# Second layer norm of a transformer block, tile by tile beside the output projection: one change to a single-core kernel

## Chip, core and metric

The kernel runs on one core of a Trainium2 chip. TensorE multiplies matrices, VectorE, ScalarE and GpSimd work beside it, SyncE issues the DMAs. Each engine takes its own instructions strictly in program order. The metric is device time in microseconds from launch to end.

## What is computed

One block over 2048 rows of 512, with 32 heads of 16, an FFN of 1792 and six modulation vectors made from c. In the kernel all products are made of fp32 parts (a high part, and a low part that is the rest).

```
mod = (silu(c) @ w_mod) -> sa, ca, ga, sb, cb, gb
h = layernorm(x) * (1 + ca) + sa
x = x + ga * (softmax(q k^T * scale) v) @ wo        # q, k, v = h @ wqkv, per head
h = layernorm(x) * (1 + cb) + sb
x = x + gb * (gelu(h @ w1 + b1) @ w2 + b2)
```

## The kernel before

Attention goes through 32 units (four blocks of 512 query rows, eight groups of four heads) of 16 key steps each. The main loop runs over these 512 **half steps** (`half_step`). Each one puts on TensorE four score tiles (`e`, line 637), four score tiles for row maxima of a later unit (`mx`, line 387) and, at its end, the four products with v of an earlier half step (`pv`, line 667). ScalarE takes the exponential of each `e` (line 642), VectorE the maximum of each `mx` (line 392). Scores contract over at most 64 rows, so two of them, or a score and a half of another product, run in the two halves of the array at a time.

Everything else is **background work**: the jobs of `work()`, of which a half step takes up to six half-array matmuls (`RUN = 6`, named `bg`, line 274), in one PSUM bank. They are, in this order, the remaining projections (`block0`), and then for query blocks 0, 1 and 2 the `front` (output projection, residual, second layer norm, transposes) and the `feed` (FFN). A job that isn't ready yields `None`: that half step has no background work and counts as idle below. Jobs that are left when the loop ends run in the **tail**, as full-array matmuls, one after the other; the fourth block's front and feed are made there by code of their own, which the change doesn't touch.

Order is set by a counter, not by time. Every `e` raises `clock["t"]` by one (a **tick**; four in a half step), and `later(n, f)` writes f's instructions n ticks further on. In the tail every second matmul is a tick.

`front(b, x2)` makes four output tiles of 128 rows (24 half matmuls, so four half steps each). For each, ScalarE copies the result out (`y`), two ticks later GpSimd adds the residual into `x2[t]`, and four ticks later VectorE takes the statistics (`ln_stat`: BN_STATS, BN_AGGR). After the last tile came one `ln_factor` for all four (VectorE adds eps, GpSimd raises to the power -0.5) and the four normalisations `xn[t]`, and the generator waited until 21 ticks were over, before `trans` turned `xn` on TensorE in four half steps (four transposes each, no other background work). Block 0's front stands alone between the projections and its FFN. The fronts of blocks 1 and 2 are put ahead of the last four groups of the FFN before them, so that their waits pass under those groups.

Of the kernel before, what the change touches and what calls it, by code (L numbers as in the profile page):

```python
# [8 lines left out]
F32 = mybir.dt.float32  # L9
FR = mybir.dt.float32r  # L10
AF = mybir.ActivationFunctionType
ALU = mybir.AluOpType
# [4 lines left out]
P = 128  # L17
# [15 lines left out]
EPS = 1e-5  # L33
# [36 lines left out]
def block_kernel(ctx: ExitStack, tc: tile.TileContext, x, wqkv, wo, w1, b1, w2, b2, c, w_mod, out):  # L70
    nc = tc.nc
    te, ve, ac, gp, sy = nc.tensor, nc.vector, nc.scalar, nc.gpsimd, nc.sync
# [21 lines left out]
    def take(name):  # L94
        ids = rings[name]
        turn[name] += 1
        return bank(ids[(turn[name] - 1) % len(ids)], name)
# [14 lines left out]
    small = ctx.enter_context(tc.tile_pool(name="small", bufs=2))  # L112
# [4 lines left out]
    mhalf = const.tile([P, NB], F32, name="mhalf")  # L117
# [7 lines left out]
    b2_b = const.tile([P, D], F32, name="b2_b")  # L125
# [107 lines left out]
    def ln_stat(mv, t, rows):  # L233
        st = small.tile([P, 6], F32, tag="bst", name="bst")
        ve.bn_stats(st, rows)  # L235
        ve.bn_aggr(mv[:, t], st)

    def ln_factor(mv, rs):
        ve.tensor_scalar(rs, mv[:, :, 1], EPS, None, op0=ALU.add)
        gp.tensor_tensor(rs, rs, mhalf, op=ALU.pow)  # L240
# [5 lines left out]
    clock = {"t": 0}  # L246
    hooks = {}

    def later(n, f):
        if n:  # L250
            hooks.setdefault(clock["t"] + n, []).append(f)
        else:
            f()
# [315 lines left out]
    for token in SCRIPT.split():  # L569
        name, ids, e, n = re.fullmatch(r"([A-Za-z]+)(\d*)(?:\.([avg]))?(?:\*(\d+))?", token).groups()  # L570
# [121 lines left out]
    def pc(b, k, a, sl=slice(None)):  # L692
        return pc_t[k][:, a, sl] if b == NB - 1 else pcs[a][:, k, sl]

    def tmp(name):
        if "f" in pools:
            return pools["f"].tile([P, D], F32, tag="t", name=name, bufs=8)
        return dvpool.tile([P, D], F32, tag="t", name=name, bufs=4)
# [50 lines left out]
    def until(cond):  # L749
        while not cond():  # L750
            yield None

    def wait(n):
        t0 = clock["t"]
        return until(lambda: clock["t"] >= t0 + n)
# [30 lines left out]
    def loaded(b, *keys):  # L786
        return until(lambda: all((b, *k) in wt for k in keys))

    def drop(b, *keys):
        used.update((b, *k) for k in keys)  # L790
# [3 lines left out]
    def o_terms(b, t, ks):  # L794
        sl = slice(t * P, (t + 1) * P)
        return [(pc(b, k, a, sl), wt[b, "o", k][:, c]) for k in ks for a, c in three]

    def load_x2(b, x2):
        for t in range(4):
            r0 = b * TB + t * P  # L800
            sy.dma_start(x2[t], x[r0 : r0 + P, :])

    def front(b, x2):


        later(9, lambda: load_x2(b, x2))
        yield from until(lambda: done[b] == KC - 1)
        yield from wait(4)
        yield from loaded(b, *[("o", k) for k in range(KC)])
        mv = small.tile([P, 4, 2], F32, tag="mv", name="mv")  # L810
        rs = small.tile([P, 4], F32, tag="rs", name="rs")
        for t in range(4):

            def evac(ps, t=t):
                y = tmp("y")
                ac.activation(y, ps, AF.Copy)  # L816

                def add():
                    gp.tensor_tensor(x2[t], y, x2[t], op=ALU.add)  # L819
                    later(4, lambda: ln_stat(mv, t, x2[t]))  # L820

                later(2, add)

            yield o_terms(b, t, range(KC)), "bg", evac
        drop(b, *[("o", k) for k in range(KC)])
        later(9, lambda: ln_factor(mv, rs))
        xn = []

        def norm(t):
            (gp if b or t in (0, 2) else ve).tensor_scalar(  # L830
                xn[t], x2[t], mv[:, t, 0:1], rs[:, t : t + 1], op0=ALU.subtract, op1=ALU.mult)

        def norms():
            xn.extend(tmp("xn") for t in range(4))
            for t in range(4):
                later(3 * (t == 3), lambda t=t: norm(t))
                later(28 + 12 * t, lambda t=t: gp.tensor_tensor(x2[t], x2[t], b2_b, op=ALU.add))

        later(13, norms)
        t0 = clock["t"]  # L840
        yield "ln"
        yield from until(lambda: clock["t"] >= t0 + 21)

        def trans(fc):
            ps = take("bg")
            for t in range(4):
                te.transpose(ps[:, t * P : (t + 1) * P], xn[t][:, fc * P : (fc + 1) * P], ident)  # L847
            h = tmp("h32")
            ac.activation(h, ps, AF.Identity, scale=modc[:, 1, fc, 0:1], bias=modc[:, 1, fc, 1:2])  # L849
            gp.tensor_copy(pc(b, fc, 0), h)  # L850
            gp.tensor_tensor(pc(b, fc, 1), h, pc(b, fc, 0).bitcast(F32), op=ALU.subtract)

        for fc in range(KC):
            yield lambda fc=fc: trans(fc)
        yield from wait(4)
# [103 lines left out]
    def work():  # L959

        yield from block0()
        fronts = [front(b, pools["x2"][b % 2]) for b in range(NB - 1)]
        for b in range(NB - 1):
            for j in fronts[b]:
                if j != "ln":
                    yield j
            for j in feed(b, pools["x2"][b % 2]):
                if j != "last":
                    togo[0] -= b == NB - 2 and j is not None
                    yield j  # L970
                elif b < NB - 2:
                    for i in fronts[b + 1]:
                        if i == "ln":
                            break
                        yield i
# [125 lines left out]
    x2 = [tpool.tile([P, D], F32, name=f"x2t{i}") for i in range(4)]  # L1101
# [21 lines left out]
    mv = small.tile([P, 4, 2], F32, tag="mv", name="mv")  # L1123
    rs = small.tile([P, 4], F32, tag="rs", name="rs")
    xn = [tmp("xn") for t in range(4)]
# [97 lines left out]
```

## Time and profile before

| | us |
|---|---|
| median of 3 runs | 1738.71 (1736.97 to 1739.3) |
| the profiled execution | 1738.16 |
| its span, first to last instruction | 1736.3 |
| TensorE, VectorE, ScalarE, GpSimd busy | 1710.8, 1375.2, 1241.8, 685.0 |

A row of the timeline has the start, the duration, the engine, the line, and what was written from what; "x8" counts instructions merged into one row, and brackets hold the idle time just ahead and what ended it. One `pv` product counts as two instructions there. The time from one `pv` row to the next is one half step. PEld is TensorE's weight load. The granted TensorE clock is 0.997 of full speed over the span.

### The profile page before, as it was taken

To read this page: it belongs to the slowest core of one execution; us is meant where nothing else is said; L and a number is where in the kernel's file an instruction comes from. 1 tells how busy PE (TensorE), PEld (TensorE's weight loads), DVE (VectorE), ACT (ScalarE), POOL (GpSimd) and SP (SyncE) were. 2 spreads that over 40 slices of the span, in tenths; PEclk is the share of its full clock that TensorE was granted. 3 is DMA by queue.
4 is the path that set the end of the run, shared out by engine and by line. 5 is a ranking of instruction groups with operands and counts; after the bars stand their busy time and mean duration, and the time that the engine had idled before them with its cause. 6 is when DMAs were issued, how large, how long until landed. Compare 5 with 4: busy or idle time off the path is not lost.

```text
span 1736.3 us, 32537 instructions
## 1 busy us (share of the span) xinstructions
PE 1710.8 (99%) x12121; PEld 891.1 (51%) x12121; DVE 1375.2 (79%) x2298; ACT 1241.8 (72%) x2379; POOL 685.0 (39%) x688
## 2 busy tenths in 40 slices
PE   7999999999999999999999999999999999999999
PEld 6654444444444444444445444444445444444777
DVE  7998888888888888888889888888888888860332
ACT  3357778778777778778777778777877778778231
POOL 7333434435121256404631356404631356525310
PEclk8999999999999999999999999999999999999999
DMA  8646776767447534335454444335364344323554
GB/s 292 205 142 200 221 218 182 236 179 223 125 136 206 125 86 117 94 85 136 113 168 106 124 114 105 94 81 166 100 174 114 101 132 114 97 66 111 195 156 166
DMA packets 137130, 251.90 MB, mean 145 GB/s; under 512 B 25854, under 2 KB 45324, under 8 KB 136972
## 3 DMA queue, kind: packets, MB, share of 16 engines
q1 hardware_dynamic: 135712, 248.19, 50.3%
q8 instruction: 96, 1.57, 0.4%
q10 hardware_dynamic: 1260, 1.63, 0.3%
q14 instruction: 62, 0.51, 0.1%
HBM read 188.49 MB, written 61.28 MB: 144 GB/s over the span
## 4 chain that ended last, share of the span: by engine, by line
PE 91%; DVE 4%; ACT 2%; POOL 1%; DMA 1%; issue 1%; SPq 0%; ACTq 0%; POOLq 0%; DVEq 0%
PE bg L274 46%; PE pv L667 29%; PE e L637 11%; PE mx L387 3%; DVE mxp L392 2%; ACT p L642 1%; PE pr L274 1%; PE o L274 1%; PE warm L438 1%; DVE hTlo L481 1%; DVE bst L235 0%; ACT h L849 0%; DMA qst<-m 0%; PE mx L333 0%; PE bg L847 0%
## 5 line engine op out<-in xcount | busy, mean ns | idle before, releaser
L392 DVE TENSOR_REDUCE mxp<-mx 128x1 f32<-128x512 f32 x2048 | 1269.4, 682 | 201.4 <-PE mx L387 182.5
L642 ACT ACTIVATE p<-e 128x512 f32<-128x512 f32 x2032 | 1064.4, 605 | 308.1 <-PE e L637 292.8
L387 PE MATMUL mx<-kh,qst 48*128 48x512 f32 x2048 | 873.3, 441 | 1.9 <-DVE mxp L392 0.4
L637 PE MATMUL e<-qst,kh 50*128 50x512 f32 x2032 | 754.6, 419 | 7.0 <-ACT p L642 6.3
L667 PE MATMUL pv<-p,vg 128*32 128x512 f32 x4096 | 546.6, 605 | 0.0
L637 PEld LDWEIGHTS e<-qst,kh 50*128 50x128 f32 x2032 | 373.7, 186 | 148.7 <-ACT p L642 141.8
L387 PEld LDWEIGHTS mx<-kh,qst 48*128 48x128 f32 x2048 | 368.6, 185 | 21.1 <-DVE mxp L392 16.2
L274 PE MATMUL bg<-w,g 64*128 64x512 f32 (+1 forms) x1044 | 277.8, 404 | 0.0
L274 PEld LDWEIGHTS bg<-w,g 64*128 64x128 f32 (+1 forms) x1044 | 183.0, 185 | 142.7 <-ACT p L642 103.3
L274 PE MATMUL bg<-pchi,w 64*128 64x512 f32 (+1 forms) x656 | 194.5, 416 | 2.1 <-ACT p L642 2.0
L274 PEld LDWEIGHTS bg<-pchi,w 64*128 64x128 f32 (+1 forms) x656 | 109.0, 184 | 150.3 <-ACT p L642 102.2
L274 PE MATMUL bg<-hThi,wqkv 64*128 64x512 f32 x560 | 167.4, 418 | 0.3 <-ACT p L642 0.3
L274 PEld LDWEIGHTS bg<-hThi,wqkv 64*128 64x128 f32 x560 | 92.8, 184 | 118.9 <-ACT p L642 106.3
L667 PEld LDWEIGHTS pv<-p,vg 128*32 128x32 f32 x4096 | 81.4, 108 | 125.4 <-issue 117.6
L884 POOL TENSOR_SCALAR s<-s 128x512 f32<-128x512 f32 x40 | 59.8, 1496 | 137.4 <-ACT s L882 127.0
L903 POOL TENSOR_TENSOR x<-y,x 128x512 f32<-128x512 f32 x28 | 35.9, 1281 | 144.3 <-ACT y L902 139.3
L274 PE MATMUL bg<-pclo,w 64*128 64x512 f32 (+1 forms) x328 | 88.6, 389 | 0.0
L872 DVE TENSOR_TENSOR g<-h,g 128x512 fp32r<-128x512 f32 x16 | 11.6, 723 | 91.5 <-PE bg L274 62.7
L274 PE MATMUL bg<-hTlo,wqkv 64*128 64x512 f32 x280 | 76.4, 392 | 0.0
L819 POOL TENSOR_TENSOR x<-y,x 128x512 f32<-128x512 f32 x12 | 15.4, 1282 | 140.9 <-ACT y L816 114.8
L274 PEld LDWEIGHTS bg<-pclo,w 64*128 64x128 f32 (+1 forms) x328 | 60.5, 184 | 12.3
L274 PE MATMUL bg<-wo,pchi 64*128 64x512 f32 x192 | 64.8, 417 | 0.0
(160 smaller groups left out, 1331.9 us busy)
## 6 DMA issues: line engine op xcount, KB each, us to landing
kh<-qk SPq DMA_DIRECT2D x256, 192.0 KB
w<-w1s SPq DMA_DIRECT2D x56, 512.0 KB
w<-w2s SPq DMA_DIRECT2D x53, 512.0 KB
vg<-v SPq DMA_DIRECT2D x64, 332.0 KB
qk<-parts SPq DMA_DIRECT2D x32, 512.0 KB
qst<-qk SPq DMA_DIRECT2D x64, 192.0 KB
qk<-parts SPq DMA_DIRECT2D x32, 256.0 KB
ou<-osb SPq DMA_DIRECT2D x32, 256.0 KB
```

The source lines that it names most:

```text
L274: return te.matmul(ps, term[0][r], term[1][r], start=i == 0, stop=i == n - 1)
L387: te.matmul(ps, qst[u][r0 : r0 + KR, p, qc * P : (qc + 1) * P], kh(u, kr // 2)[r0 : r0 + KR, p, (kr % 2) * TB : (kr % 2 + 1) * TB], start= ...
L392: ins = ve.tensor_reduce(mxp[u][:, hc, kr : kr + 1], ps, axis=AX.X, op=ALU.max, negate=True)
L438: te.matmul(warm[:, :P], ident, ident, start=True, stop=True)
L481: e.tensor_tensor(hT[b][1][:, f], keep.pop(("H", b, f)), hT[b][0][:, f].bitcast(F32), op=ALU.subtract)
L637: te.matmul(ps, kh(u, kc // 8)[r0 : r0 + KX, p, (kc % 8) * P : (kc % 8 + 1) * P], qst[u][r0 : r0 + KX, p], start=True, stop=True)
L642: saw(ac.activation(t, ps, AF.Exp, scale=SCALE))
L667: te.matmul(cur["ps"][32 * j : 32 * (j + 1)], vg[u][:, kc, j * VW : j * VW + 32], pt.pop(4 * s + j), start=kc == 0, stop=kc == NKC - 1)
L819: gp.tensor_tensor(x2[t], y, x2[t], op=ALU.add)
L872: ve.tensor_tensor(g[:, 1], h, g[:, 0].bitcast(F32), op=ALU.subtract)
L884: gp.tensor_scalar(s, s, 1.0, None, op0=ALU.add)
L903: later(4, lambda: gp.tensor_tensor(x2[t], y, x2[t], op=ALU.add))
```

## The change

Each tile gets statistics, factor and normalisation of its own as soon as it is there. The factors are four 128x1 tiles (`rt`) in place of one 128x4. Tiles 0 to 2 are normalised by GpSimd, tile 3 by VectorE, in every block (before: block 0 by GpSimd for tiles 0 and 2 and VectorE for 1 and 3, the other blocks by GpSimd alone). The last tile's steps follow each other one tick sooner. The transposes come when all four tiles are written and nine ticks are over. The adding of b2 to `x2[t]` now comes 40 ticks after the tile's normalisation.

```
-        rs = small.tile([P, 4], F32, tag="rs", name="rs")
+        def norm(t):
+            xn[t] = tmp("xn")
+            (gp if t < 3 else ve).tensor_scalar(
+                xn[t], x2[t], mv[:, t, 0:1], rs[t], op0=ALU.subtract, op1=ALU.mult)
+            later(40, lambda: gp.tensor_tensor(x2[t], x2[t], b2_b, op=ALU.add))
+        def stat(t):
+            ln_stat(mv, t, x2[t])
+            later(2 if t < 3 else 1, lambda: factor(t))
+        def factor(t):
+            rs[t] = small.tile([P, 1], F32, tag=f"rt{t}", name=f"rt{t}")
+            ve.tensor_scalar(rs[t], mv[:, t, 1:2], EPS, None, op0=ALU.add)
+            gp.tensor_tensor(rs[t], rs[t], mhalf[:, 0:1], op=ALU.pow)
+            later(3 if t < 3 else 2, lambda: norm(t))
...
-                    later(4, lambda: ln_stat(mv, t, x2[t]))
+                    later(4 if t < 3 else 3, lambda: stat(t))
...
-        later(9, lambda: ln_factor(mv, rs))
-        def norm(t):
-            (gp if b or t in (0, 2) else ve).tensor_scalar(
-                xn[t], x2[t], mv[:, t, 0:1], rs[:, t : t + 1], op0=ALU.subtract, op1=ALU.mult)
-        def norms():
-            xn.extend(tmp("xn") for t in range(4))
-            for t in range(4):
-                later(3 * (t == 3), lambda t=t: norm(t))
-                later(28 + 12 * t, lambda t=t: gp.tensor_tensor(x2[t], x2[t], b2_b, op=ALU.add))
-        later(13, norms)
...
-        yield from until(lambda: clock["t"] >= t0 + 21)
+        yield from until(lambda: len(xn) == 4 and clock["t"] >= t0 + 9)
```

VectorE in block 0's front, from the statistics of tile 3 (`x_7490`) on. First before, then changed; `mxp` rows are the row maxima of the main loop, `mn` the end of a unit's maxima:

```order
L235 BN_STATS bst<-x_7490 128x6
L236 BN_AGGR mv<-bst 128x2
L392 TENSOR_REDUCE mxp<-mx 128x1 x5
L239 TENSOR_SCALAR rs<-mv 128x4
L392 TENSOR_REDUCE mxp<-mx 128x1 x4
L830 TENSOR_SCALAR xn<-x_7488,mv,rs 128x512
L392 TENSOR_REDUCE mxp<-mx 128x1 x3
L830 TENSOR_SCALAR xn<-x_7490,mv,rs 128x512
```

In the changed kernel:

```order
L235 BN_STATS bst<-x_7490 128x6
L236 BN_AGGR mv<-bst 128x2
L392 TENSOR_REDUCE mxp<-mx 128x1
L826 TENSOR_SCALAR rt_8356<-mv 128x1
L392 TENSOR_REDUCE mxp<-mx 128x1 x2
L816 TENSOR_SCALAR xn<-x_7490,mv,rt_8356 128x512
```

Tile 3 is normalised after three maxima in place of twelve, and tile 1's normalisation has left VectorE.

GpSimd at the same place, from the residual add of tile 3 on, before:

```order
L819 TENSOR_TENSOR x_7490<-y,x_7490 128x512
L240 TENSOR_TENSOR rs<-rs,mhalf 128x4
L830 TENSOR_SCALAR xn<-x_7487,mv,rs 128x512
L830 TENSOR_SCALAR xn<-x_7489,mv,rs 128x512
L850 CAST pchi_5322<-h_8532 128x512
```

And changed, where `b_b` is b2 over all rows and the `xn` rows of tiles 0 to 2 stand further up, each behind its own add:

```order
L837 TENSOR_TENSOR x_7490<-y,x_7490 128x512
L818 TENSOR_TENSOR x_7487<-x_7487,b_b 128x512
L827 TENSOR_TENSOR rt_8356<-rt_8356,mhalf 128x1
L854 CAST pchi_5322<-h_8439 128x512
L855 TENSOR_TENSOR pclo_5323<-h_8439,pchi_5322 128x512
```

Between the add and the cast that follows the first transposes, GpSimd now has one add of b2 and one 128x1 power.

TensorE where the main loop ends and the tail begins. Before: the last two `pv` products stand together, and two FFN groups of 12 (`pchi`, `pclo`) follow:

```order
L274 MATMUL bg<-pclo_5323,w_22538 128x512 x3
L637 MATMUL e<-qst,kh_192 128x512
L667 MATMUL pv<-p,vg 32x512 x8
L274 MATMUL bg<-pchi_5322,w_22566 128x512 x8
L274 MATMUL bg<-pclo_5323,w_22566 128x512 x4
L274 MATMUL bg<-pchi_5322,w_22629 128x512 x8
L274 MATMUL bg<-pclo_5323,w_22629 128x512 x4
L274 MATMUL bg<-w_22693,g 128x512 x3
```

Changed:

```order
L637 MATMUL e<-qst,kh_192 128x512 x2
L667 MATMUL pv<-p,vg 32x512 x4
L274 MATMUL bg<-pchi_5322,w_22563 128x512 x2
L274 MATMUL bg<-pclo_5323,w_22563 128x512 x4
L667 MATMUL pv<-p,vg 32x512 x4
L274 MATMUL bg<-pchi_5322,w_22620 128x512 x8
L274 MATMUL bg<-pclo_5323,w_22620 128x512 x4
L274 MATMUL bg<-w_22688,g 128x512 x3
```

Of the two FFN groups one has gone into the loop, but for its last six half matmuls, which now stand alone between the last two `pv` products. In the rows of TensorE as a whole, block 0 has three idle half steps between its projection and its first transposes where it had six; the idle half steps of the other two blocks are as many as before, and stand three half steps sooner.

More of the change, by code (lines that the diff above doesn't have):

```diff
@@ L810, in front @@
         mv = small.tile([P, 4, 2], F32, tag="mv", name="mv")
-        rs = small.tile([P, 4], F32, tag="rs", name="rs")
+        rs = {}
+        xn = {}
+        def norm(t):
[11 more added lines that the diff above has]
+            later(3 if t < 3 else 2, lambda: norm(t))
         for t in range(4):
@@ L825, in front @@
         drop(b, *[("o", k) for k in range(KC)])
-        later(9, lambda: ln_factor(mv, rs))
-        xn = []
-        def norm(t):
-            (gp if b or t in (0, 2) else ve).tensor_scalar(
-                xn[t], x2[t], mv[:, t, 0:1], rs[:, t : t + 1], op0=ALU.subtract, op1=ALU.mult)
-        def norms():
-            xn.extend(tmp("xn") for t in range(4))
-            for t in range(4):
-                later(3 * (t == 3), lambda t=t: norm(t))
-                later(28 + 12 * t, lambda t=t: gp.tensor_tensor(x2[t], x2[t], b2_b, op=ALU.add))
-        later(13, norms)
         t0 = clock["t"]
         yield "ln"
-        yield from until(lambda: clock["t"] >= t0 + 21)
+        yield from until(lambda: len(xn) == 4 and clock["t"] >= t0 + 9)
         def trans(fc):
```

## The prediction

> **What bounds the kernel now.** I read the page first: its engine totals, then the chain that ended last.
>
> ```profile
> PE 1710.8 (99%) x12121; PEld 891.1 (51%) x12121; DVE 1375.2 (79%) x2298; ACT 1241.8 (72%) x2379; POOL 685.0 (39%) x688
> PE 91%; DVE 4%; ACT 2%; POOL 1%; DMA 1%; issue 1%; SPq 0%; ACTq 0%; POOLq 0%; DVEq 0%
> ```
>
> TensorE carries 91% of the chain. So a wait that is taken out pays only by what TensorE has less to do, or waits less, afterwards. Next I took TensorE's timeline around block 0's front, keeping the `pv` rows, one for each half step. The first two bound a half step with background work; from 585.23 on there is none, until the transposes.
>
> ```profile
> 561.71 1.06 PE L667 MATMUL pv<-p,vg 128*32 128x512 f32 x8
> 564.63 1.07 PE L667 MATMUL pv<-p,vg 128*32 128x512 f32 x8
> ...
> 585.23 1.06 PE L667 MATMUL pv<-p,vg 128*32 128x512 f32 x8
> 587.97 1.06 PE L667 MATMUL pv<-p,vg 128*32 128x512 f32 x8
> 591.15 1.06 PE L667 MATMUL pv<-p,vg 128*32 128x512 f32 x8
> 593.89 1.07 PE L667 MATMUL pv<-p,vg 128*32 128x512 f32 x8
> ...
> 602.32 1.07 PE L667 MATMUL pv<-p,vg 128*32 128x512 f32 x8
> 603.33 0.65 PE L847 MATMUL bg<-ident,xn 128*128 128x128 f32 x4
> ```
>
> A half step with background work takes 564.63 - 561.71 = 2.92 us, an idle one 587.97 - 585.23 = 2.74: an idle half step is nearly as long as a full one. The six idle ones take 602.32 - 585.23 = 17.09 us. The one that holds tile 3's statistics takes 3.18. So what is lost in an idle half step is not its 2.74 us, but six half matmuls that must be done later. Where they are done is the tail. The timeline there, all engines, at the first groups of FFN weights `w` with `g`:
>
> ```profile
> 1677.96 16.50 PE L274 MATMUL bg<-w,g 128*128 128x512 f32 x72
> ```
>
> 72 full matmuls in 16.50 us, 0.229 each, with no wait inside. VectorE's rows from the front to the transposes, and one half step of the loop without a front:
>
> ```profile
> 588.60 0.68 DVE L235 BATCH_NORM_STATS2 bst<-x 128x6 f32<-128x512 f32 x1
> 589.32 0.18 DVE L236 BATCH_NORM_AGGREGATE mv<-bst 128x2 f32<-128x6 f32 x1
> 592.38 0.16 DVE L239 TENSOR_SCALAR rs<-mv 128x4 f32<-128x4 f32 x1
> 595.12 0.54 DVE L830 TENSOR_SCALAR xn<-x,mv,rs 128x512 f32<-128x512 f32 x1
> 597.37 0.54 DVE L830 TENSOR_SCALAR xn<-x,mv,rs 128x512 f32<-128x512 f32 x1
> ...
> 1300.39 2.48 DVE L392 TENSOR_REDUCE mxp<-mx 128x1 f32<-128x512 f32 x4 [0.43 <-PE mx L387]
> ```
>
> Four maxima take 2.48 us, and VectorE then waits 0.43 for TensorE: that is the room for layer-norm work in a full half step.
>
> **The change, part by part.** By the rows of the changed program, three of block 0's six idle half steps go. All later background work comes three half steps, that is 18 half matmuls, sooner. Twelve of them are half of an FFN group, six more stand at the loop's end, and the tail loses that one group of 12 full matmuls.
>
> *Tail.* 12 x 0.229 = -2.75 us.
>
> *Loop.* The three idle half steps that stay hold tile 3's statistics, factor and one normalisation. I take 2.74 + 3.18 + 2.85 = 8.77 for them (the last with 0.11 for a normalisation, from the other half steps of the six: 17.09 - 2.74 - 3.18 - 2.74 = 8.43 for three with two normalisations in them). So 17.09 - 8.77 = 8.32 go, and three full ones come, 3 x 2.92 = 8.76: +0.44. Bounds 0 to +0.6.
>
> *The end of the loop.* ScalarE's second half of the GELU is written ten ticks behind its FFN group. TensorE's and ScalarE's rows there:
>
> ```profile
> 1605.66 1.11 PE L667 MATMUL pv<-p,vg 128*32 128x512 f32 x8
> 1607.80 0.62 ACT L882 ACTIVATE s<-s 128x512 f32<-128x512 f32 x1
> 1608.38 1.06 PE L667 MATMUL pv<-p,vg 128*32 128x512 f32 x8
> 1611.61 2.67 PE L667 MATMUL pv<-p,vg 128*32 128x512 f32 x16
> 1613.22 0.14 PEld L667 LDWEIGHTS pv<-p,vg 128*32 128x32 f32 x4 [0.61 <-ACT p L642]
> 1614.21 2.11 PE L274 MATMUL bg<-pchi,w 128*128 128x512 f32 x8
> ```
>
> Behind that tanh the half step takes 1611.61 - 1608.38 = 3.23 in place of 1608.38 - 1605.66 = 2.72, since no maxima are left and the exponentials set the pace. Shifted by three half steps, one more of them falls into the loop: +0.51 (0 to +1.0).
>
> *The six half matmuls left over.* They stand between the last two `pv` products and run alone in half the array. The spacing of background matmuls and the turn from and to `pv`, in TensorE's rows ahead of the 564.63 above:
>
> ```profile
> 562.71 0.50 PE L274 MATMUL bg<-wo,pchi 64*128 64x512 f32 x1
> ...
> 563.04 0.39 PE L274 MATMUL bg<-wo,pchi 64*128 64x512 f32 x1
> ...
> 563.28 0.39 PE L274 MATMUL bg<-wo,pclo 64*128 64x512 f32 x1
> ...
> 564.22 0.48 PE L387 MATMUL mx<-kh,qst 48*128 48x512 f32 x1
> ```
>
> One goes each 0.24 us (563.28 - 563.04); the first after `pv` takes 0.33, the last before `pv` 0.41. Six alone: 0.33 + 4 x 0.24 + 0.41 = 1.7 us. Part of this covers what TensorE now spends waiting there: the last two `pv` take 2.67 against two at 1.06, 0.55 of waiting, with the exponential there at 1613.2. That leaves +1.1 (0 if the wait hides more than I see, +1.7 if none). The Trainium skill, TensorEngine Tiling (Array Packing), Key Properties, says that a change of tiling mode drains TensorE. The trace agrees: 0.33 and 0.41 at the turns against 0.24 between; without the drain this term would be 6 x 0.24 - 0.55 = +0.9 and the sum 0.2 lower.
>
> *VectorE, other blocks.* Each front gets three more small factor ops and blocks 1 and 2 a normalisation that GpSimd had. Their statistics rest in full half steps:
>
> ```profile
> 917.33 1.07 PE L667 MATMUL pv<-p,vg 128*32 128x512 f32 x8
> 920.34 1.06 PE L667 MATMUL pv<-p,vg 128*32 128x512 f32 x8
> ```
>
> With statistics of 0.68 + 0.18 the half step takes 3.01, 0.09 more than 2.92, though VectorE had only 0.43 free: the rest is taken up by its lag. Nine factor ops of 0.16 each and two normalisations of 0.54 are 2.5 us of VectorE work; tile 3's come within two half steps (0.86 + 0.16 + 0.54 = 1.56 against 2 x 0.43), so there I take 0.3 a block. Sum +0.6 (0 to 2.5).
>
> *GpSimd and the order in queues.* The rows of before, and those of the factors by tile:
>
> ```profile
> 585.81 1.28 POOL L819 TENSOR_TENSOR x<-y,x 128x512 f32<-128x512 f32 x1 [10.50 <-ACT y L816]
> 592.62 1.04 POOL L240 TENSOR_TENSOR rs<-rs,mhalf 128x4 f32<-128x4 f32 x1 [5.53 <-DVE rs L239]
> 593.77 4.60 POOL L830 TENSOR_SCALAR xn<-x,mv,rs 128x512 f32<-128x512 f32 x2
> ...
> L1143 POOL TENSOR_TENSOR rs<-rs,mhalf x4: 548/572/870, 1640.3 to 1646.6; 128x1 f32<-128x1 f32 x4
> ```
>
> GpSimd normalises tiles 0 to 2 under the projection, four half steps apart, where it idles 10.50 us between adds: nothing. For tile 3 the chain is add (to 587.09), statistics, factor, power (0.57), normalisation. With one maximum between, the factor is ready by about 590, the power by 590.8 (b2's add of tile 0, 1.28, ends before that) and `xn` by 591.9. TensorE comes to the transposes at 593.89 + 1.0 = 594.9, or a few tenths earlier. If the 2.7 us or so of cover were gone, TensorE would stand at the head of its queue with the scores and `pv` products behind it, and ScalarE and VectorE would wait for those.
>
> The sum is -2.75 + 0.44 + 0.51 + 1.1 + 0.6 = -0.1 us. The profiled execution took 1738.16, 0.55 under the median of the three runs and within them: **1738.1 us**.
>
> **The rivals.** *The pieces at the loop's end hide better.* Without the leftover's 1.1, and with nothing lost on VectorE, -0.1 - 1.1 - 0.6 = -1.8: 1736.4. For it speaks that TensorE does wait on ScalarE there; against it, that the wait seen is 0.55.
>
> *The tail can't use the time (the other side).* The tail's weights come by a queue whose issues are set by ticks behind the loop's end. TensorE would reach the fourth block's output projection 2.75 us sooner after that end, and could then wait for it. Rows of SyncE and TensorE, VectorE's last part of the attention result, and a stretch of the table of windows (its last two columns are the share of the DMA engines and GB/s):
>
> ```profile
> 1625.02 1.69 SPq L782 DMA_DIRECT2D wt<-wos x3
> ...
> 1628.62 0.69 DVE L735 TENSOR_TENSOR kh<-ob,kh 128x512 fp32r<-128x512 f32 x1
> ...
> 1633.44 4.25 PE L274 MATMUL o<-wt,kh 128*128 128x512 f32 x18
> ...
> 1630.00:1635.00 5.00, 5.00 (x23) 4.13 (x22) 1.90 (x3) 0.00 (x0) 0.00 (x0) 1.00 1.02 408
> ```
>
> The attention result is there at 1629.3, 4 us ahead. The weights were issued at 1625.02 into DMA engines that are full at 408 GB/s, and used at 1633.44 without a wait; when they landed the rows don't say. The rival decides if they land less than 2.75 us before that; at worst all of it is lost: -0.1 + 2.75 = +2.65, 1740.8. Against it: one 512 KB slice of w2 now goes out before the loop's end, which takes 0.52 / 0.408 = 1.3 us from the queue ahead of them. The Trainium skill, DMA: Bandwidth & Descriptors, Where 436 GB/s comes from, puts HBM's limit for a core at about 358 GB/s. Here 408 was measured, so that limit doesn't hold; with it the slice ahead would be worth an estimated 1.5 us, and the rival's sum would be the same.
>
> *Tile 3 comes late.* TensorE waits at the transposes; it needs a chain 2.7 us longer than worked out, say by VectorE lagging behind its maxima by a half step. Two us more make 1740.
>
> *The three half steps come back as idle ones later.* Then the tail stays and only VectorE's +0.6 is left: 1738.8. The rows of the changed TensorE speak against it: as many idle half steps in blocks 1 and 2, one group fewer in the tail.
>
> **How the numbers follow.** Forecast 0.60, the better cover 0.17, the tail 0.14, tile 3 late 0.05, idle again 0.02; 0.02 for the rest. About 0.2% (3.5 us) is what a measurement of this kernel can tell from no change, and all of these lie inside it. Outside are only their far ends: the better cover together with the lower bounds of the loop terms, or the lost tail together with VectorE's 2.5 us. That gives 0.08 faster, 0.09 slower, 0.83 within. The range takes the two middle rivals' sums and the spread of the runs (2.3 us in all): 1735.6 to 1740.9.
>
> **What would show it.** Right: 10.5 us or less from the last output projection's `pv` to the first transpose (17.09 + 1.0 now); a `pv` row of the loop's end 1.7 us apart from the last, with six `bg` between; the tail from the first full matmul to the span's end 2.75 us shorter than now. Wrong: TensorE idle at `ident,xn` released by VectorE; a `o<-wt,kh` row with DMA as its releaser; half steps of more than 3.2 us where tile 3 of blocks 1 and 2 is normalised; a span changed by over 3 us either way.

## The result, and the profile after

The changed kernel takes **1730.69 us** (median of 5 runs, 1730.26 to 1731.28) against 1738.52 of the kernel before (5 runs, 1736.70 to 1739.30): ratio 0.9957, interval 0.9945 to 0.9968. The forecast was 1738.1, its range 1735.6 to 1740.9: the kernel became faster by some 8 us where no change was forecast. The profiled execution took 1730.26, span 1728.4, granted TensorE clock 0.999 (0.997 before; another of the five runs had 0.996 and took 1730.39, so the clock isn't it).

The page of the changed kernel, engine totals and chain:

```profile
PE 1699.9 (98%) x12133; PEld 890.7 (52%) x12133; DVE 1375.0 (80%) x2307; ACT 1246.1 (72%) x2379; POOL 694.7 (40%) x703
PE 91%; DVE 3%; DMA 2%; ACT 2%; POOL 1%; issue 1%; SPq 0%; ACTq 0%; DVEq 0%; POOLq 0%
```

TensorE still carries 91% of the chain; the other engines' busy times hardly changed, but TensorE's fell by 10.9 us though it does the same products. Block 0's front in TensorE's timeline (`pv` rows, and the first transpose):

```profile
584.06 1.06 PE L667 MATMUL pv<-p,vg 128*32 128x512 f32 x8
586.80 1.06 PE L667 MATMUL pv<-p,vg 128*32 128x512 f32 x8
590.03 1.07 PE L667 MATMUL pv<-p,vg 128*32 128x512 f32 x8
592.88 1.06 PE L667 MATMUL pv<-p,vg 128*32 128x512 f32 x8
593.88 0.66 PE L851 MATMUL bg<-ident,xn 128*128 128x128 f32 x4
```

Three idle half steps, 592.88 - 584.06 = 8.82 us (8.77 forecast), and the transposes follow at once. So much came as predicted. To see where the 8 us are I cut both timelines at the same four places. The rows that are new here are the first `pv` and the last `mx`, of the kernel before and then of the changed one:

```profile
112.25 1.07 PE L667 MATMUL pv<-p,vg 128*32 128x512 f32 x8
...
1548.76 0.47 PE L387 MATMUL mx<-kh,qst 48*128 48x512 f32 x1
```

```profile
111.15 1.07 PE L667 MATMUL pv<-p,vg 128*32 128x512 f32 x8
...
1540.43 0.73 PE L387 MATMUL mx<-kh,qst 48*128 48x512 f32 x2
```

(The last of the changed kernel's two merged `mx` starts at 1540.77.) The last column compares two runs that are described under the experiments.

| stretch | change, measured | forecast | the same change with the ScalarE wait out of both kernels (e5 against e6) |
|---|---|---|---|
| start to the first `pv` | -1.10 | 0 | +0.11 |
| first `pv` to block 0's first transpose | -8.35 | -8.32 | -8.28 |
| first transpose to the last `mx` (three full half steps more, VectorE) | **+1.47** | +8.76 + 0.6 | +10.40 |
| last `mx` to the first full matmul | +0.35 | +0.51 + 1.1 | +1.58 |
| tail | -0.27 | -2.75 | -1.60 |
| sum | -7.90 | -0.1 | +2.21 |

The first stretch differs from execution to execution (111.15 to 113.64 over all that were profiled, whatever the kernel), so its -1.10 is not put down to the change. The loop behind the transposes should have grown by 9.4 us and grew by 1.5. Within it, half steps alternate. TensorE's `e` and `pv` rows, and ScalarE's exponentials, of two neighbours in the changed kernel:

```profile
696.57 1.07 PE L667 MATMUL pv<-p,vg 128*32 128x512 f32 x8
697.91 0.39 PE L637 MATMUL e<-qst,kh 50*128 50x512 f32 x1
...
698.84 0.64 PE L637 MATMUL e<-qst,kh 50*128 50x512 f32 x2
699.42 1.07 PE L667 MATMUL pv<-p,vg 128*32 128x512 f32 x8
700.76 0.39 PE L637 MATMUL e<-qst,kh 50*128 50x512 f32 x1
...
701.69 0.71 PE L637 MATMUL e<-qst,kh 50*128 50x512 f32 x2
...
702.34 1.06 PE L667 MATMUL pv<-p,vg 128*32 128x512 f32 x8
```

```profile
698.34 1.12 ACT L642 ACTIVATE p<-e 128x512 f32<-128x512 f32 x2 [0.78 <-PE e L637]
...
701.25 1.09 ACT L642 ACTIVATE p<-e 128x512 f32<-128x512 f32 x2 [0.23 <-PE e L637]
```

The first half step takes 2.85 us, the second 2.92. In the first, ScalarE starts its exponential 0.43 us behind the start of the first `e` (698.34 - 697.91), in the second 0.49 (701.25 - 700.76). The fourth `e` of a half step writes into the bank of the first (three banks), so it waits for that exponential, and what is late there is handed on to the next `pv`. I count the half steps between 2.8 and 3.0 us by what stands ahead of their first exponential, the separate wait that is explained next. Before, 435 have it there and take 2.915 on average; 6 haven't. In the changed kernel 281 have it and take 2.914, and 149 haven't and take 2.854; 147 of these 149 lie behind the first transpose.

What differs is in the instruction list of ScalarE. Two half steps of exponentials from the FFN of block 0, first before, then changed, with what each waits for (Activation is ScalarE itself, and `p` is one of ten tiles that hold exponentials):

```
L642 ACTIVATE p_10469<-e_10467 128x512 [waits PE_49,Activation_49]
L642 ACTIVATE p_10478<-e_10476 128x512 [waits PE_49]
L642 ACTIVATE p_10487<-e_10485 128x512 [waits PE_49]
L642 ACTIVATE p_10493<-e_10489 128x512 [waits PE_49]
L642 ACTIVATE p_10512<-e_10510 128x512 [waits PE_49,Activation_49]
L642 ACTIVATE p_10521<-e_10519 128x512 [waits PE_49,Activation_49]
L642 ACTIVATE p_10530<-e_10528 128x512 [waits PE_49]
L642 ACTIVATE p_10536<-e_10532 128x512 [waits PE_49]
```

```
L642 ACTIVATE p_10139<-e_10137 128x512 [waits PE_49]
L642 ACTIVATE p_10151<-e_10149 128x512 [waits PE_49,Activation_49]
L642 ACTIVATE p_10160<-e_10158 128x512 [waits PE_49]
L642 ACTIVATE p_10166<-e_10162 128x512 [waits PE_49]
L642 ACTIVATE p_10184<-e_10182 128x512 [waits PE_49,Activation_49]
L642 ACTIVATE p_10193<-e_10191 128x512 [waits PE_49]
L642 ACTIVATE p_10202<-e_10200 128x512 [waits PE_49]
L642 ACTIVATE p_10208<-e_10204 128x512 [waits PE_49]
```

An exponential that waits for two engines is two instructions here: a **separate wait** for the `e` product, and the exponential itself with the wait for ScalarE's own earlier write of that `p` tile. In the trace's records the separate wait is 0.017 us long and starts 0.062 us ahead of the exponential's start. Ahead of the first exponential it delays the half step: over the whole changed kernel the first exponential starts 0.496 us (median) behind its `e` with it and 0.435 without. On the second exponential it costs nothing that can be seen; the exponentials queue behind one another there. Which exponential needs it depends on how long ago the free tile it gets was last written (the ten `p` tiles come free in the order in which `pv` reads them). In these two lists the first or second exponential has the separate wait where its tile was written 10 exponentials ago or fewer, and hasn't where it was 11 or more. Before, the first exponentials get tiles written 10 and 8 exponentials ago, in turn; after the shift by an odd number of half steps they get 11 and 9. Over the whole program 482 half steps have a separate wait ahead of their first exponential before, 315 after: 167 x 0.062 = 10.4 us, and the loop and its end fell short of the forecast by 7.9 + 1.3 = 9.2.

The Trainium skill, Perfetto Trace Analysis, Per-engine timelines, has a mechanism that fits: an instruction of the sequencer alone holds the sequencer until its semaphores are met, and only then is the next one fetched and decoded, while an activation that carries its wait itself stands decoded in a wait queue. It gives no price; the trace's records give 0.06 us. That the delay is this decoding isn't shown here.

The tail is the other miss. TensorE and the SyncE queue of the changed kernel there:

```profile
1618.04 2.28 SPq L782 DMA_DIRECT2D wt<-wos  x4
...
1621.67 1.56 PE L274 MATMUL bg<-wt,g 128*128 128x512 f32 x6
...
1624.30 0.96 PE L274 MATMUL o<-wt,kh 128*128 128x512 f32 x3 [1.07 <-DMA wt<-wos]
1625.59 0.98 PE L274 MATMUL o<-wt,kh 128*128 128x512 f32 x3 [0.32 <-DMA wt<-wos]
1626.87 9.83 PE L274 MATMUL o<-wt,kh 128*128 128x512 f32 x42 [0.30 <-DMA wt<-wos]
```

The group of 12 is gone, but the output projection now waits for Wo three times, 1.69 us in the brackets. In starts of rows, at 0.229 a matmul, it is more: 1.26 behind the six `bg`, then 0.60 and 0.59 behind three `o` each. These 2.45 leave 0.30 of the 2.75, and 0.27 was measured. The loop's end came as forecast: six `bg` between the last two `pv`, which are 2.60 apart, of which 1605.58 - 1603.98 = 1.60 for the six (1.7 forecast).

```profile
1602.98 1.06 PE L667 MATMUL pv<-p,vg 128*32 128x512 f32 x8
1603.98 0.74 PE L274 MATMUL bg<-pchi,w 64*128 64x512 f32 x2
1604.56 1.09 PE L274 MATMUL bg<-pclo,w 64*128 64x512 f32 x4
1605.58 1.06 PE L667 MATMUL pv<-p,vg 128*32 128x512 f32 x8
1606.58 2.11 PE L274 MATMUL bg<-pchi,w 128*128 128x512 f32 x8
```

### The profile page after: what moved, and what is told of

Same layout as the page of the kernel before. It is cut to its first block, busy times and chain, and to the rows that moved or that the text cites. A ratio compares the mean times of both kernels' runs of the same rounds, so it can differ in the third digit from the quotient of the medians.

```text
span 1728.4 us, 32510 instructions
## 1 busy us (share of the span) xinstructions
PE 1699.9 (98%) x12133; PEld 890.7 (52%) x12133; DVE 1375.0 (80%) x2307; ACT 1246.1 (72%) x2379; POOL 694.7 (40%) x703
## 4 chain that ended last, share of the span: by engine, by line
PE 91%; DVE 3%; DMA 2%; ACT 2%; POOL 1%; issue 1%; SPq 0%; ACTq 0%; DVEq 0%; POOLq 0%
PE bg L274 46%; PE pv L667 29%; PE e L637 11%; PE mx L387 3%; DVE mxp L392 2%; PE pr L274 1%; ACT p L642 1%; PE o L274 1%; DMA wm<-in_w_mod_dram 0%; DMA wt<-wos 0%; ACT h L853 0%; PE mx L333 0%; PE bg L851 0%; DMA rden<-dn 0%; DVE bst L235 0%
## 5 line engine op out<-in xcount | busy, mean ns | idle before, releaser
L907 POOL TENSOR_TENSOR x<-y,x 128x512 f32<-128x512 f32 x28 | 36.0, 1287 | 153.5 <-ACT y L906 153.5
L876 DVE TENSOR_TENSOR g<-h,g 128x512 fp32r<-128x512 f32 x15 | 10.9, 725 | 88.1 <-ACT g L875 88.1
L881 POOL TENSOR_TENSOR s<-h 128x512 f32<-128x512 f32 x41 | 42.7, 1042 | 47.7 <-ACT h L880 47.6
```

Source lines behind the costliest of these rows:

```text
L876: ve.tensor_tensor(g[:, 1], h, g[:, 0].bitcast(F32), op=ALU.subtract)
L881: gp.tensor_tensor(s, h, h, op=ALU.mult)
L907: later(4, lambda: gp.tensor_tensor(x2[t], y, x2[t], op=ALU.add))
```

## The experiments

Theory A: the separate wait ahead of a half step's first exponential costs 0.06 us, and the change took it away from every second one by shifting an odd number of half steps. Rival B: the sooner transposes or the new layer norm gained the time. Rival C: the order of halves and banks that goes with the parity. The runs e1 to e4, e5 to e8 and e9 to e10 are three groups, each on one chip together with the kernel before.

**Shifts and halves (e1 to e4).** Four kernels; the kernel before beside them took 1738.26 (1736.1 to 1739.63).

e1, the changed kernel:

```
-        yield from until(lambda: len(xn) == 4 and clock["t"] >= t0 + 9)
+        yield from until(lambda: len(xn) == 4 and clock["t"] >= t0 + 13)
```

> The changed kernel with its wait four ticks longer (13 in place of 9): block 0's transposes come two half steps sooner than in the kernel before, not three. Theory A (a separate wait instruction): where ScalarE gets a wait of its own ahead of the first exponential of a half step, that half step takes 0.06 us longer; an odd shift takes this instruction away from every second half step, an even one doesn't. In the program 484 half steps have it here, 482 before, 315 in the changed kernel. A expects the gain gone: 1730.7 + 169 x 0.062 = 1741, with some 2 us less if an idle half step costs nothing: 1738 to 1742. Theory B (the transposes that come sooner, and the layer norm beside the projection, are what was gained): two thirds of the gain stay, 1732 to 1734.

Measured 1740.92 (1739.36 to 1742.42), ratio 1.0018, interval 1.0009 to 1.0027. As A expects: with an even shift all of the gain is gone, and the kernel is slower than before.

e2, the kernel before:

```
-        yield from until(lambda: clock["t"] >= t0 + 21)
+        yield from until(lambda: clock["t"] >= t0 + 25)
```

> The kernel before with its wait four ticks longer (25 in place of 21), the layer norm as it was: one more idle half step, an odd shift the other way. Theory A: 313 half steps have the separate wait in place of 482, so 1738.5 - 169 x 0.062 = 1728 and about half a us for the later background work: 1727 to 1730, faster although TensorE idles longer. Theory B: a longer idle stretch, 1739 to 1741.

Measured 1733.32 (1732.29 to 1734.2), ratio 0.9972, interval 0.9962 to 0.9983. The direction is A's: an idle half step more makes the kernel faster, and every second half step behind the front takes 2.86 us. The size was off: the tail took 125.10 us in place of 122.14, one group of 12 matmuls (2.75) that the half step later sends there, which the expectation left out.

e3, the kernel before:

```
-        h = hs % 2
-        if h or len(wt) < len(used) + KC:
+        h = 1 - hs % 2
+        if hs % 2 or len(wt) < len(used) + KC:
```

> The kernel before with the two halves of the array exchanged for the background work of all half steps (h = 1 - hs % 2; the loading of weights keeps its own order); layer norm and waits as before. Theory A: 238 half steps with the separate wait in place of 482, also in the first projections: 1738.5 - 244 x 0.062 = 1723.4 (1721 to 1726). Theory B: 1738.5, as before.

Measured 1723.73 (1722.45 to 1724.43), ratio 0.9916, interval 0.9902 to 0.9929: A's 1723.4, with the old layer norm and the old wait. B can't give that.

e4, the changed kernel:

```
-        h = hs % 2
-        if h or len(wt) < len(used) + KC:
+        h = (hs + (hs < 165)) % 2
+        if hs % 2 or len(wt) < len(used) + KC:
```

> The changed kernel with the halves exchanged only up to the idle stretch of block 0 (hs < 165), so that the projections too start with the other half. Theory A: 239 half steps with the separate wait in place of 315: 1730.7 - 76 x 0.062 = 1726.0 (1725 to 1728), better than both kernels. Theory B: 1730.7, as the changed kernel.

Measured 1728.91 (1724.85 to 1730.16), ratio 0.9945, interval 0.9932 to 0.9957. Just above A's range. In the profiled execution the stretch from the first `pv` to the first transpose fell from 482.73 to 478.53 us, 4.2 of the 4.7 expected; its first `pv` came 1.5 us later than in the changed kernel's, which hides a part.

**The wait itself (e5 to e7).** The halves, the parity and the order of work stay; only the choice among the free `p` tiles changes. e5 is made from the changed kernel, e6 from the kernel before, by the same edit:

```
+    p_free = [(-1, ppool.tile([P, TB], F32, tag=f"p{i}", name="p", bufs=1)) for i in range(10)]
+    p_at = [0]
+    def p_take():
+        p_free.sort(key=lambda f: f[0])
+        k = p_at[0]
+        p_at[0] += 1
+        return k, p_free.pop(0 if k % 4 != 1 else -1)[1]
...
-            t = ppool.tile([P, TB], F32, tag="p", name="p")
+            k, t = p_take()
...
+            p_free.append(done_p)
```

> The changed kernel with the ten tiles for the exponentials (p) handed out by hand: the second exponential of a half step takes the free tile that was written last, the others the one written longest ago. Order of work, waits of the layer norm and halves of the array as in the changed kernel; only 1 half step has the separate wait before its first exponential in place of 315 (380 exponentials still have one, at the second place). Theory A (the separate wait ahead of the first exponential costs 0.06 us): 1730.7 - 314 x 0.062 = 1711, or up to 1714 where ScalarE isn't what TensorE waits for. Theory C (the separate wait only goes along with the parity; what costs is the order of halves and banks): 1730.7 within 1.5.

> The kernel before with its p tiles handed out by the same rule: 1 half step with the separate wait in place of 482. Theory A: 1738.3 - 481 x 0.062 = 1708.5, up to 1711.5. With the wait out of the way on both sides, what is left between this and the changed kernel with the same rule is the layer norm's change itself; by the stages of the two traces (loop +2.65 as forecast, tail -0.3) this one is 2 to 3 us faster. Theory C: 1738.3 within 1.5, and the changed kernel stays 7 us faster.

e7 is e5 with the rule turned round:

```
-        return k, p_free.pop(0 if k % 4 != 1 else -1)[1]
+        return k, p_free.pop(0 if k % 4 else -1)[1]
```

> The changed kernel with the p tiles handed out the other way round: the first exponential of a half step takes the free tile that was written last. The same parity and order as the changed kernel, but 486 half steps have the separate wait ahead of the first exponential. Theory A: 1730.7 + 171 x 0.062 = 1741 (1739 to 1743), slower than the kernel before. Theory C: 1730.7 within 1.5.

With 1738.56 (1737.36 to 1740.63) of the kernel before beside them: e5 1714.19 (1713.87 to 1714.56), ratio 0.9860, interval 0.9846 to 0.9873; e6 **1712.62** (1711.61 to 1714.07), ratio 0.9851, interval 0.9838 to 0.9865; e7 1739.41 (1738.34 to 1742.63), ratio 1.0006, interval 0.9997 to 1.0015. `pv` rows of e6, then of e7:

```profile
697.17 1.07 PE L676 MATMUL pv<-p,vg 128*32 128x512 f32 x8
...
700.02 1.07 PE L676 MATMUL pv<-p,vg 128*32 128x512 f32 x8
```

```profile
704.36 1.07 PE L676 MATMUL pv<-p,vg 128*32 128x512 f32 x8
707.27 1.06 PE L676 MATMUL pv<-p,vg 128*32 128x512 f32 x8
```

2.85 in e6, 2.91 in e7. e7 is as slow as the kernel before. The time follows the number of half steps whose first exponential has the separate wait (1 against 486), and C falls: with the same parity and order, e5 and e7 lie 25 us apart. e5 and e6 stayed 3 and 4 us short of the full counts of 1711 and 1708.5, and lie 0.2 and 1.1 us above A's ranges: the wait costs a half step slightly less than 0.062. The 435 half steps of the kernel before with it take 2.915, those of e6 between 2.8 and 3.0 us 2.857; that makes 25 us, the loop's end gives 1.3 (64.12 in place of 65.45), and 25.9 were measured. The group rows of the weight loads of `e` (behind the second bar stands the idle time ahead of them, by releaser) for the kernel before, the changed one and e5 say the same from TensorE's side:

```profile
L637 PEld LDWEIGHTS e<-qst,kh 50*128 50x128 f32 x2032 | 373.7, 186 | 148.7 <-ACT p L642 141.8 <-issue 2.0 <-DMA qst<-m 1.0
```

```profile
L637 PEld LDWEIGHTS e<-qst,kh 50*128 50x128 f32 x2035 | 374.2, 186 | 135.7 <-ACT p L642 128.5 <-issue 2.0 <-ACT y L906 1.7
```

```profile
L645 PEld LDWEIGHTS e<-qst,kh 50*128 50x128 f32 x2035 | 374.9, 186 | 118.8 <-ACT p L650 109.0 <-issue 2.0 <-ACT y L916 1.7
```

e6 beats both kernels, by 26 and 18 us. And with the tiles out of the comparison **the change gains nothing**: e5's median is 1.6 us above e6's (their intervals overlap), and stretch by stretch the profiled executions say +2.2 (the table's last column).

**The tail (e8).** e5, and in `o_prep`, when the loop is over:

```
             if over[0]:
-                wload()
+                for _ in range(3):
+                    wload()
...
-                for _ in range(6):
+                for _ in range(4):
                     wload()
```

> The changed kernel with p tiles by the rule that frees the first exponential, and in the tail two more weight loads in front of the last denominators' return, so that the first slice of Wo is asked for about 3 us sooner. In the changed kernel's tail TensorE waits 1.07 + 0.32 + 0.30 us for Wo. Theory T (the tail's gain of 2.75 went into this wait): 1.2 to 2.5 us less than the changed kernel with the rule alone, and no o row released by a DMA. Rival (the DMA engines are full there, so what is asked for sooner only delays the attention result): the same, or up to 1 us more.

Measured 1714.81 (1713.24 to 1718.15): no gain against e5's 1714.19. The output projection's rows:

```profile
1608.38 0.86 PE L274 MATMUL o<-wt,kh 128*128 128x512 f32 x3
1610.20 0.96 PE L274 MATMUL o<-wt,kh 128*128 128x512 f32 x3 [0.96 <-DMA wt<-wos]
1611.48 9.80 PE L274 MATMUL o<-wt,kh 128*128 128x512 f32 x42 [0.32 <-DMA wt<-wos]
```

The first slice is there in time, but it already was in e5, whose first `o` row stands without a wait and whose second and third wait 0.33 and 0.31: theory T's 1.2 to 2.5 us were reckoned from the changed kernel's three waits, and there was less to gain. The second slice now comes later, 0.96 of waiting in place of 0.33. So asking for one slice sooner doesn't cure the wait, and the rival fits; only that one slice was asked for much sooner (2.9 us; the other three 0.65).

**The end of a unit (e9).** In e5 the half step at a unit's end takes 3.00 us, in e6 2.88 (medians of 20). ScalarE and the `pv` rows of e5 there:

```profile
1130.56 0.59 ACT L916 ACTIVATE y<-bg 128x512 f32<-128x512 f32 x1
1131.04 1.10 ACT L650 ACTIVATE p<-e 128x512 f32<-128x512 f32 x2
1131.99 0.63 ACT L662 ACTIVATE osb<-pv 128x512 f32<-128x512 f32 x1
```

```profile
1130.60 1.07 PE L676 MATMUL pv<-p,vg 128*32 128x512 f32 x8
1133.60 1.07 PE L676 MATMUL pv<-p,vg 128*32 128x512 f32 x8
```

A group's copy `y` and the unit's copy `osb` fall into one half step, 1130.60 to 1133.60, and the exponentials queue behind both. e9 is e5 with the edit of e1:

> The changed kernel with the p tiles by the rule that frees the first exponential, and the wait four ticks longer (13 in place of 9): the background work comes two half steps sooner than before, not three. With the rule, parity should no longer matter. In the changed kernel with the rule the half step that ends a unit (each 16th) takes 3.00 us, against 2.88 in the kernel before with the rule: there a projection group's copy by ScalarE falls together with the copy of the unit's attention result. Theory U (the phase of the groups against the units does that): with a shift of two the half step at a unit's end goes back to 2.86 to 2.90, and from the first transpose to the last maximum takes about 928.3 + 2 x 2.86 + 0.3 = 934.3 us, not 936.9. Rival (the new layer norm itself makes it longer): 3.00 stays. In both the total is 1713 to 1717, since the tail has a rest of twelve half matmuls more.

Measured 1713.77 (1712.12 to 1715.22; kernel before 1737.36), within both totals. The stretch decides: 933.16 us from the first transpose to the last `mx` (934.3 and 936.9 expected), and 2.85 to 2.89 in nearly all half steps at a unit's end. So a shift by three half steps, in a pattern of four, also moved the groups' ends onto the units' ends: 0.12 us at each.

**Where the first `e` stands (e10).** The kernel before:

```
-            if e_ok(a) and (sum(ec) < ne - 1 and k % 2 == 1 or ...
+            if e_ok(a) and (sum(ec) < ne - 1 and k % 2 == 0 or ...
```

> The kernel before with one number changed: in a half step with background work the scores for the exponentials (e) go beside the first, third and fifth background matmul, not beside the second, fourth and sixth. The p tiles are as before: 482 half steps have the separate wait ahead of the first exponential, and other exponentials get 445 more of them. Theory A2 (0.06 us are lost only because first e, first exponential and fourth e are the chain that TensorE waits for; the first e comes 0.23 us sooner now, more than the 0.06): 1738.5 - 482 x 0.06 = 1710, up to 1716. Rival (each separate wait costs ScalarE 0.06 us and with it the half step, wherever it stands): 1738.5 or more, up to 1738.5 + 445 x 0.06 = 1765.

Measured 1773.55 (1772.54 to 1777.18), ratio 1.0206, interval 1.0191 to 1.0221: outside both. TensorE's scores and VectorE's maxima in one half step:

```profile
801.42 0.50 PE L637 MATMUL e<-qst,kh 50*128 50x512 f32 x1
801.76 0.40 PE L387 MATMUL mx<-kh,qst 48*128 48x512 f32 x1
802.21 1.89 DVE L392 TENSOR_REDUCE mxp<-mx 128x1 f32<-128x512 f32 x3 [0.48 <-PE mx L387]
802.91 0.40 PE L637 MATMUL e<-qst,kh 50*128 50x512 f32 x1
802.96 0.50 PE L387 MATMUL mx<-kh,qst 48*128 48x512 f32 x1
```

The full half steps take 2.97, with two separate waits or with three (165, 101 and 129 half steps in three patterns, each with a mean of 2.97), which speaks against the rival. These patterns all have one ahead of the first exponential; only four full half steps haven't, too few to tell. That the chain through the exponential is no longer the limit, as A2 says, is seen in the weight loads of `e`, which wait 22.4 us for exponentials in place of 141.8:

```profile
L637 PEld LDWEIGHTS e<-qst,kh 50*128 50x128 f32 x2032 | 372.8, 185 | 47.0 <-ACT p L642 22.4 <-issue 2.0 <-ACT y L902 1.7
```

But the first `mx` now comes later, VectorE's first maximum ends at about 802.9, and the fourth `mx`, which takes the bank of the first, starts right there. That this second chain sets the 2.97 is read from these rows, not tried.

## Why the prediction was wrong

- **The step that failed** is the loop term: "three full ones come, 3 x 2.92 = 8.76". It took a full half step for a constant, and the half steps behind the three had no term at all. All of them were shifted too, and 2.92 held 0.06 us of a separate wait on ScalarE that depends on the parity of the shift. That was worth about -9 to -10 us, against a sum of -0.1. e1, e2, e3, e5, e6 and e7 show it, in both directions.
- **Idle half steps**: -8.32 forecast, -8.35 and -8.28 measured. **Loop's end**: +1.61 forecast, +1.58 with the wait out of both kernels (+0.35 with it, as these half steps gained too).
- **VectorE and what else slows the loop**: +0.6 forecast. With the wait out, the loop grew by 10.40, of which three half steps are 3 x 2.857 = 8.57; 1.83 is left, and e6 has one half step of 4.35 us in that stretch that e5 hasn't (1.49 over the others; TensorE waits there for the DMA that brings a unit's row maxima, `qst<-m`). With that one set apart, about 3.3 were added; whether it is gone because of the change wasn't tried. In e9 the same sum is 933.16 - 928.32 = 4.84 for two half steps of 2.857, and with the 1.49 set apart 0.6 is left, the size that the prediction put down. So most of the 3.3 lies at the ends of units, a place that the prediction didn't name, and comes by the shift of three, not by VectorE. The sign that the prediction gave for VectorE, a half step over 3.2 us at tile 3 of block 1 or 2, shows once in the changed kernel: 3.23, with the statistics of block 1.
- **Tail**: -2.75 forecast, -0.27 (e5 against e6: -1.60) measured. The rival "the tail can't use the time" gave the right mechanism, a wait for Wo (its sign, an `o` row released by a DMA, shows three times), and the wrong end: its +2.65 stood on a loop without a gain. Each short wait cost more than its bracket says: the second `o` row comes 1.29 us behind the first, three matmuls are 3 x 0.229 = 0.69, so 0.60 was lost where 0.32 is shown. In e5 the first wait is missing and the other two cost 0.57 + 0.59 = 1.16, which leaves 1.59 of the 2.75. e8 shows that asking for the first slice sooner doesn't buy the rest back.
- **A count** in the prediction is short: the group that left the tail is 24 half matmuls, 18 in the three half steps and six more at the loop's end, not twelve and six. TensorE has 12133 - 12121 = 12 instructions more, 24 halves for 12 full ones. The sum doesn't hang on it.
- Without the wait on both sides the change comes out at +1.6 us (e5 against e6; +2.2 in the profiled executions), where the sum said -0.1 and the range reached to +2.8. Against that sum the loop costs 1.0 more (2.5, were it not for e6's one long half step) and the tail 1.1 more. That the rest still falls into the range is partly luck.

## What to carry to other kernels

When a change shifts a repeating pattern, first ask what else has a period: the tiles of a ring, the array's halves, the ends of groups and units; compare the instruction lists, waits included, one period before and one after, since a half step's duration is only a constant if its waits are the same. Here the chain from TensorE to ScalarE and back to TensorE, through a ring of three banks, paid for each wait instruction ahead of its first link, though ScalarE was busy 72% of the time. And before a gain is credited to a change, repeat it with the accident removed on both sides: here that turned -8 us into no gain (about +2), and left a kernel 26 us faster than before in which the layer norm is the old one.

## What the runs showed of the hardware

A separate wait on ScalarE, 0.017 us long in the trace's records, delays an exponential that stands at the head of its half step by 0.06 us (0.496 against 0.435 behind its `e`); 486 of them against 1 in the place that matters made 25 us (e7 against e5). On the second exponential of a half step it costs nothing that can be seen: in e5 half steps between 2.8 and 3.0 us with it there take 2.857 (328 of them), those without any 2.864 (103).
